# Reordering the low-rank adds of a gated-attention and channel-mixer kernel, and storing its last outputs singly

## The chip, the cores and the metric

The kernel runs on one core of a Trainium2 chip. A profile is one execution with every instruction's start and duration. PE is the matrix engine, DVE the vector engine, ACT the scalar engine, POOL and SP are engines that here mostly issue transfers. A label such as L545 is a line of the kernel's source.

## The reference, cut to what matters

For each of 8 batches of 3136 rows, with D = 256, a rank of 32 and 1024 hidden channels:

```python
scores = (1.0 / S) * z @ z.T
x = u * (np.maximum(scores, 0) ** 2 @ v)          # gated attention
h = (x.T @ U @ V).T                               # low-rank mix over rows
y = x + h
out = y + np.maximum(y @ w_ch1, 0) @ w_ch2        # channel mixer
```

## The kernel before: the parts concerned

A batch is done in 25 turns i of 128 rows (one of 64), two turns to an output pair. While batch b is in attention, the low-rank adds and the channel mixer of batch b - 1 are woven in. PSUM is the memory that the matmuls write and that DVE and ACT read here; a bank is one tile of 128 x 512 float32 in it. Four PSUM banks form two sets of two: an output pair accumulates in one set, and the low-rank product and the down matmuls use the other, until the next pair opens on it. Here are the low-rank add of one chunk (up to four tiles of rows), and the score, whose activation and square are queued by ACT and DVE when the matmuls are queued:

```python
def low_rank(b, c, ps=None, turned=True):
    ps = spare() if ps is None else ps            # the set that no pair accumulates in
    # ... two to four matmuls into ps[0], ps[1]                    (L531, PE)
    for h in range(2):                            # one add per bank
        # ...
        nc.vector.tensor_tensor(out=q, in0=split(ps[h][:, ...]), in1=q, op=ALU.add)   # L545, DVE
    if turned:
        turn_x(b, c)                              # DMA transpose, for the up matmuls

def score(b, parts):
    # ... two matmuls into one of two double banks                 (L298, PE)
    for dst, src in todo:
        nc.scalar.activation(out=dst, in_=src, func=AF.Relu, scale=sc)          # L311, ACT
    for dst, _ in todo:
        nc.vector.tensor_tensor(out=dst, in0=dst, in1=dst, op=ALU.mult)         # L313, DVE
```

The weaving of a turn, where `main` holds the 25 steps of one output tile (two matmuls each) and `fill` the scores that are due; `_spread` deals the fill out evenly between the steps:

```python
ahead = dict(zip((2, 3, 6, 7, 10, 11, 14), range(NC)))   # turn -> chunk
# ...
main = attend_steps(b, o)
if b and i in ahead:
    main.insert(17 if (i + (i > FIRST)) % 2 == 0 else 10, lambda c=ahead[i]: low_rank(b - 1, c))
_spread(main, fill)
```

Turn 7 has three scores; the second falls due after step index 12. The last batch has no following batch to hide in, so its ups, downs and low-rank adds stand at the end:

```python
rank(b, other[0], 0, NT - 3)
run(late[: NH // 2])                  # relus of the first chunk, alternating between bank sets
rank(b, other[0], NT - 3)
run(late[NH // 2 : NH // 2 + 1])
mix(b, 0)
run(late[NH // 2 + 1 :])
low_rank(b, 1, other)
for c in range(NC + 1):
    up, down = last[c]
    if c + 2 < NC:
        up.insert(3 if c == 0 else 1, lambda c=c: low_rank(b, c + 2, other))
    if c == 0:
        up.insert(1, lambda: low_rank(b, 0, None, False))
    run(_merge(up, down))
```

## Time and profile before

| | before |
|---|---|
| median time, first three runs | 1004.49 us (1002.80 to 1008.39) |
| median of all six runs of the first comparison | 1003.74 us |
| span of the profiled run, granted clock | 1003.0 us, 1.000 |
| PE idle in it | 18.8 us |
| shortest interval between two batches | 121.21 us |
| first last-batch rank matmul (L462) to start of the last relu | 50.80 us |
| start of the last relu to the end of the span | 6.57 us |

The last three rows are from the trace's instruction records, and they serve as rulers. The interval is that between the first L479 matmuls (the rank projection, once a batch) of neighbouring batches; the shortest of the six is free of stray waits.

### The profile page before, as it was taken

How to read it: one execution, taken by the hardware profiler on the slowest of the kernel's cores; microseconds unless marked ns; L12 is line 12 of the kernel's file. 1: busy time of each engine (PE TensorE's matmuls, PEld its weight loads, DVE VectorE, ACT ScalarE, POOL GpSimd, SP SyncE). 2: the span in 40 equal slices, each digit the busy share in tenths (PEclk: the TensorE clock that was granted, in tenths of full speed). 3: DMA queues.
4: the chain of work that ended last, by engine and by line, in shares of the span. 5: the costliest groups of instructions: out<-in, count | busy, mean ns of one | idle time of the engine just before them, and what ended most of it. 6: DMA issues, size and time to landing. Idle time of an engine off the chain costs nothing.

```text
span 1003.0 us, 31017 instructions
## 1 busy us (share of the span) xinstructions
PE 984.2 (98%) x13688; PEld 776.2 (77%) x13688; DVE 550.6 (55%) x1002; ACT 612.3 (61%) x835; POOL 171.8 (17%) x317
## 2 busy tenths in 40 slices
PE   7899999999999999999999999999999999999998
PEld 5678777787778877788787887778878788777855
DVE  6868754457544665456644566445663457542342
ACT  7877764667645776466755667466664667633154
POOL 5111112111121211221112211112111120011000
PEclk9999999999999999999999999999999999999999
DMA  9999989999798999999999997989989998678442
GB/s 177 186 196 206 175 153 186 169 198 173 149 205 165 170 160 181 178 179 168 156 185 174 188 162 149 192 177 179 170 156 181 181 183 152 127 152 166 99 98 97
DMA packets 414646, 167.94 MB, mean 167 GB/s; under 512 B 389472, under 2 KB 399136, under 8 KB 414512
## 3 DMA queue, kind: packets, MB, share of 16 engines
q1 hardware_dynamic: 385280, 99.68, 62.9%
q0 software_dynamic: 29232, 66.28, 28.5%
q8 instruction: 107, 1.75, 0.7%
q14 instruction: 27, 0.22, 0.1%
HBM read 61.88 MB, written 25.69 MB: 87 GB/s over the span
## 4 chain that ended last, share of the span: by engine, by line
PE 90%; DVE 4%; ACT 3%; DMA 2%; issue 0%; POOL 0%; DVEq 0%; ACTq 0%; POOLq 0%
PE ps L371 46%; PE ps L608 17%; PE ps L563 17%; PE ps L298 6%; ACT A L311 3%; DVE A L313 1%; PE ps L405 1%; DMA strip<-A 1%; DVE x_bf L545 1%; PE ps L531 1%; DMA z_c<-in_z_dram 1%; PE ps L479 1%; DMA zT<-z_bf 1%; DVE both L386 1%; DVE x_bf L395 0%
## 5 line engine op out<-in xcount | busy, mean ns | idle before, releaser
L311 ACT ACTIVATE A<-ps 128x832 bf16<-128x832 f32 (+9 forms) x477 | 359.1, 768 | 156.1 <-PE ps L298 149.6
L371 PE MATMUL ps<-v,A 64*128 64x256 bf16 x4988 | 341.8, 270 | 2.4 <-DVE A L313 1.1
L313 DVE TENSOR_TENSOR A<-A 128x832 bf16<-128x832 bf16 (+9 forms) x477 | 244.6, 527 | 131.2 <-ACT A L311 128.0
L371 PE MATMUL ps<-v,strip 64*128 64x256 bf16 x4420 | 307.4, 269 | 3.6 <-DMA strip<-A 2.7
L371 PEld LDWEIGHTS <-A 64*128 64x128 bf16 x4988 | 246.8, 94 | 45.8 <-issue 11.2
L581 ACT ACTIVATE relu_bf<-ps 128x1024 bf16<-128x1024 f32 (+2 forms) x206 | 186.0, 911 | 140.8 <-PE ps L563 138.7
L371 PEld LDWEIGHTS <-strip 64*128 64x128 bf16 x4420 | 222.8, 94 | 37.4 <-DMA strip<-A 4.6
L619 DVE TENSOR_TENSOR o_sb<-ps,x_bf 128x512 f32<-128x512 f32 (+1 forms) x104 | 69.7, 670 | 246.2 <-PE ps L608 223.8
L608 PE MATMUL ps<-w_bf,relu_bf 128*128 128x256 bf16 (+1 forms) x1600 | 201.5, 273 | 0.2 <-ACT relu_bf L579 0.2
L563 PE MATMUL ps<-ut,w_bf 128*128 128x512 bf16 (+2 forms) x896 | 198.3, 353 | 1.1 <-DVE x_bf L545 1.0
L608 PEld LDWEIGHTS <-relu_bf 128*128 128x128 bf16 (+1 forms) x1600 | 152.3, 98 | 46.6 <-issue 4.6
L563 PEld LDWEIGHTS <-w_bf 128*128 128x128 bf16 x896 | 85.0, 98 | 63.4 <-issue 7.7
L355 POOL DMA_DIRECT2D u_sb<-in_u_dram x96 | 53.7, 559 | 456.1 <-DVE x_bf L395 440.8
L298 PE MATMUL ps<-zT 64*128 64x416 bf16 (+8 forms) x812 | 131.7, 312 | 0.0
L385 ACT COPY both<-ps 128x512 f32<-128x512 f32 (+1 forms) x104 | 58.9, 566 | 73.8 <-PE ps L371 66.4
L632 POOL DMA_DIRECT2D out_dram<-o_sb x84 | 46.0, 548 | 278.2 <-DVE o_sb L619 274.9
L386 DVE TENSOR_TENSOR both<-ps,both 128x512 f32<-128x512 f32 (+1 forms) x104 | 69.4, 667 | 27.5 <-ACT both L385 26.7
L395 DVE TENSOR_TENSOR x_bf<-both,u_sb 128x512 bf16<-128x512 f32 (+1 forms) x104 | 69.8, 672 | 3.6
L545 DVE TENSOR_TENSOR x_bf<-ps,x_bf 128x512 bf16<-128x512 f32 (+1 forms) x112 | 65.4, 626 | 8.1 <-PE ps L531 8.0
L298 PEld LDWEIGHTS <-zT 64*128 64x128 bf16 x812 | 43.2, 94 | 3.9
L244 POOL DMA_DIRECT2D v<-in_v_dram x61 | 34.1, 561 | 1.2 <-DMA w_bf<-in_moe_w_ch_dram 1.1
L298 PE MATMUL ps<-relu_bf 64*128 64x416 bf16 (+9 forms) x121 | 22.2, 332 | 4.1 <-ACT A L311 3.3
(54 smaller groups left out, 207.9 us busy)
## 6 DMA issues: line engine op xcount, KB each, us to landing
u_sb<-in_u_dram POOLq DMA_DIRECT2D x96, 256.0 KB, 4.1
out_dram<-o_sb POOLq DMA_DIRECT2D x84, 256.0 KB, 3.2
v<-in_v_dram POOLq DMA_DIRECT2D x57, 192.0 KB, 5.1
strip<-A SPq DMA_TRANSPOSE x196, 5.6
out_dram<-o_sb SPq DMA_DIRECT2D x12, 256.0 KB, 2.0
z_c<-in_z_dram POOLq DMA_DIRECT2D x7, 384.0 KB, 5.7
u_sb<-in_u_dram POOLq DMA_DIRECT2D x16, 64.0 KB, 2.9
ut<-x_bf SPq DMA_TRANSPOSE x56, 3.6
```

The costliest lines, as they stand in the source:

```text
L298: mm(out=ps[:, k, :n], lhsT=zT[halves[k], j, :], rhs=zT_flat[halves[k], c : c + n], start=True, stop=True,)
L311: nc.scalar.activation(out=dst, in_=src, func=AF.Relu, scale=sc)
L313: nc.vector.tensor_tensor(out=dst, in0=dst, in1=dst, op=ALU.mult)
L371: mm(out=acc[t0][h][:, (o - t0) * D : (o - t0 + 1) * D], lhsT=w[halves[h]], rhs=v_both[b % 2][halves[h], j, :], start=start, stop=stop, **kw,)
L385: nc.scalar.copy(out=both[:, :w], in_=banks[1][:, :w])
L386: nc.vector.tensor_tensor(out=both[:, :w], in0=banks[0][:, :w], in1=both[:, :w], op=ALU.add)
L395: nc.vector.tensor_tensor(out=x_at(b, t0, n), in0=split(both[:, :w]), in1=u_sb[:, :n, :].rearrange("p t (a c) -> p t a c", c=P), op=ALU.mult,)
L545: nc.vector.tensor_tensor(out=q, in0=split(ps[h][:, : len(ks) * D]), in1=q, op=ALU.add)
L563: mm(out=ps[i][:, :w] if apart else ps[:, i, :w], lhsT=w1_bf[:, db, (hp + i) * P : (hp + i + 1) * P], rhs=uT[c][:, db, len(chunks[c]) * P ...
L581: nc.scalar.activation(out=relus[c][:, hp : hp + 2, :w], in_=ps[:, :, :w], func=AF.Relu)
L608: mm(out=ps[r, k * D : (k + 1) * D], lhsT=relus[c][:, ht, q : q + (TAIL if two else P)], rhs=w2_bf[:, ht, :], start=(ht < 1 + two), stop=( ...
L619: nc.vector.tensor_tensor(out=o_sb[:p, :nk, :].rearrange("p t (a c) -> p t a c", c=P), in0=split(ps[:p, : nk * D]), in1=x_at(b, t, nk)[:p] ...
```

## The change

Its intent: in the last batch, spread the low-rank adds so that they use one bank set (`other`) and stay out of the way of the first chunk's relus; let the last two output tiles leave one by one; and put the add of turn 7 later, away from the wait in front of it. The diff, cut to its core:

```diff
+        apart = b == B - 1 and c == NC - 1          # in down_steps
...
-            if k == len(pair) - 1:
-                t, nk = pair[0], len(pair)
-                o_sb = out_pool.tile([P, 2, D], FP32, name="o_sb")
+            if apart or k == len(pair) - 1:
+                k0 = k if apart else 0
+                t, nk = pair[k0], k + 1 - k0
+                if k0 == 0:
+                    hold[1] = out_pool.tile([P, 2, D], FP32, name="o_sb")
+                o_sb = hold[1][:, k0 : k + 1, :]
...
-                    in0=split(ps[:p, : nk * D]),
+                    in0=split(ps[:p, k0 * D : (k + 1) * D]),
...
-                main.insert(17 if (i + (i > FIRST)) % 2 == 0 else 10, lambda c=ahead[i]: low_rank(b - 1, c))
+                at = 17 if (i + (i > FIRST)) % 2 == 0 else 13 if i == 7 else 10
+                main.insert(at, lambda c=ahead[i]: low_rank(b - 1, c))
...
+    ups = NH // 2
     rank(b, other[0], 0, NT - 3)
-    run(late[: NH // 2])
+    run(late[: ups // 2])
     rank(b, other[0], NT - 3)
-    run(late[NH // 2 : NH // 2 + 1])
+    run(late[ups // 2 : ups])
     mix(b, 0)
-    run(late[NH // 2 + 1 :])
     low_rank(b, 1, other)
+    run(late[ups:])
     for c in range(NC + 1):
         up, down = last[c]
-        ...                                         # the inserts shown above
+        steps = _merge(up, down)
+        adds = {0: ((2, 2),), 1: ((0, 1), (3, 5))}.get(c, ((c + 2, 2),) if c + 2 < NC else ())
+        for n, at in reversed(adds):
+            steps.insert(at, lambda n=n: low_rank(b, n, other, n > 0))
+        run(steps)
```

More of the change, by code (lines that the diff above doesn't have):

```diff
@@ L614, in step @@
                 )
-            if k == len(pair) - 1:
-                t, nk = pair[0], len(pair)
-                o_sb = out_pool.tile([P, 2, D], FP32, name="o_sb")
+            if apart or k == len(pair) - 1:
[4 more added lines that the diff above has]
+                o_sb = hold[1][:, k0 : k + 1, :]
                 p = P if t < NF else TAIL
                 nc.vector.tensor_tensor(
-                    out=o_sb[:p, :nk, :].rearrange("p t (a c) -> p t a c", c=P),
-                    in0=split(ps[:p, : nk * D]),
+                    out=o_sb[:p].rearrange("p t (a c) -> p t a c", c=P),
+                    in0=split(ps[:p, k0 * D : (k + 1) * D]),
                     in1=x_at(b, t, nk)[:p],
@@ L631, in step @@
                 if t < NF:
-                    store(out=rows(out[b])[:, t : t + nk, :], in_=o_sb[:, :nk, :])
+                    store(out=rows(out[b])[:, t : t + nk, :], in_=o_sb)
                 else:
@@ L896 @@
     other = sets[opened[0] % 2]
+    ups = NH // 2
     rank(b, other[0], 0, NT - 3)
-    run(late[: NH // 2])
+    run(late[: ups // 2])
     rank(b, other[0], NT - 3)
-    run(late[NH // 2 : NH // 2 + 1])
+    run(late[ups // 2 : ups])
     mix(b, 0)
-    run(late[NH // 2 + 1 :])
     low_rank(b, 1, other)
+    run(late[ups:])
     for c in range(NC + 1):
         up, down = last[c]
-        if c + 2 < NC:
-            up.insert(3 if c == 0 else 1, lambda c=c: low_rank(b, c + 2, other))
-        if c == 0:
-            up.insert(1, lambda: low_rank(b, 0, None, False))
-        run(_merge(up, down))
+        steps = _merge(up, down)
[3 more added lines that the diff above has]
+        run(steps)
 _INS = ['u', 'v', 'z', 'moe_U', 'moe_V', 'moe_w_ch1', 'moe_w_ch2']
```

## The prediction

> **What bounds the kernel now.** I read the page's busy times and chain first.
>
> ```profile
> PE 984.2 (98%) x13688; PEld 776.2 (77%) x13688; DVE 550.6 (55%) x1002; ACT 612.3 (61%) x835; POOL 171.8 (17%) x317
> ...
> PE 90%; DVE 4%; ACT 3%; DMA 2%; issue 0%; POOL 0%; DVEq 0%; ACTq 0%; POOLq 0%
> ```
>
> The matrix engine (PE) is busy for 984.2 of 1003.0 us, and 90% of the chain is its matmuls. The change removes no matmul, so at most the 18.8 us of PE idleness (1.9%) is to be had. Hence I look only for moments where PE waits. The list of waits names one that repeats once in each of seven batches:
>
> ```profile
> PE ps L531 <- DVE x_bf L545: 1.1, 7, 0.2
> ```
>
> The timeline around the first of them (microseconds from the start, then duration):
>
> ```profile
> 138.39 1.28 DVE L545 TENSOR_TENSOR x_bf<-ps,x_bf 128x512 bf16<-128x512 f32 x2
> ...
> 139.30 0.27 PE L531 MATMUL ps<-t_sb,V_bf 64*128 64x256 bf16 x1
> ...
> 139.72 0.28 PE L531 MATMUL ps<-t_sb,V_bf 64*128 64x256 bf16 x2 [0.16 <-DVE x_bf L545]
> ...
> 140.05 0.33 PE L298 MATMUL ps<-zT 64*128 64x352 bf16 x2
> ...
> 140.19 1.02 DVE L545 TENSOR_TENSOR x_bf<-ps,x_bf 128x512 bf16<-128x512 f32 x2
> ...
> 140.42 0.76 ACT L311 ACTIVATE A<-ps 128x704 bf16<-128x704 f32 x1 [0.71 <-PE ps L298]
> ...
> 141.21 0.96 DVE L313 TENSOR_TENSOR A<-A 128x704 bf16<-128x704 bf16 x2
> ...
> 141.56 0.72 PE L371 MATMUL ps<-v,A 64*128 64x256 bf16 x10
> ```
>
> L531 is the low-rank product of chunk 3 of the previous batch, at turn i = 7. It writes the pair of PSUM banks that the accumulation is not using. Its second matmul waits until the vector engine (DVE) has read the previous low-rank result out of its bank (L545, ends 139.67). Three such matmuls take about 0.22 us elsewhere; here 0.54 us pass (139.30 to 139.84), so 0.32 us are lost. Note the last line: at 141.56 the next output pair (i = 8) opens **the same two banks**. Its matmuls also wait for L545, which ended at 141.21: a margin of 0.35 us.
>
> The last batch is the other place. From the chain of waits, in order of time:
>
> ```profile
> 949.02 0.39 ACT relu_bf L579
> ...
> 952.00 0.68 DVE o_sb L619
> 952.68 0.91 DVE x_bf L545 x2
> 953.59 0.20 issue
> 953.79 0.69 DVE x_bf L545
> 954.49 0.04 issue
> 954.53 0.59 PE ps L563 x2
> ...
> 998.96 0.69 DVE o_sb L619
> ```
>
> Between 947 and 955 us the chain leaves PE for relus and adds. The largest hole is before 954.53: chunk 0's second relu pair (L563) needs the banks into which low_rank(0) has just been put, and DVE reaches its two adds after three others. From 958 us on PE is packed. At the end one 0.69 us add is followed by the last store.
>
> **What the Trainium skill says.** "PSUM — Partial Sum Buffer", section "Engine vs sequencer instructions": VectorE queues are strict FIFO, and matmuls start and complete in program order. The trace agrees: at 139.72 the third L531 matmul, whose bank was free, waited behind the second. "VectorE: DVE Perf Modes", section "The TRN2 errata": a fixed cost per instruction, and (N+151)/0.96 ns for an fp32 tensor_tensor. The trace has 0.69 us for 512 columns and 0.42 us for the 64x256 output add, which is what that gives; half an add is not half the time. "DMA: Bandwidth & Descriptors", section "Latency and other measured facts": about 2 us of fixed cost per DMA. The 256 KB stores land 2.0 us after issue, and the DMA view of the last 7 us shows the engines moving data for about 0.8 us of that, so size matters less than the fixed part. "Perfetto Trace Analysis", section "Identifying the Most-Contended Engine", says that matmul busy time is a poor measure of headroom; I use it only to locate gaps, and issue starts for sizes.
>
> **The change part by part.** I read the order of instructions per engine in both built programs.
>
> *Part 1, spread low-rank adds (last batch).* The same matmuls and adds stand in another order. Walk, with durations of the trace (four 512-column matmuls 0.86 us, eight L608 0.87, a low-rank group with its changes of shape 0.42). The last ranks move between the two halves of chunk 0's first relus, so the t1 copy comes earlier and the 0.27 us wait at 949.19 to 949.46 shrinks; the mix issues at 949.2 instead of 950.4. low_rank(1) follows it; then sixteen down matmuls run from 949.85 (relu ends about 949.80) to 951.6, and chunk 0's up starts there instead of 952.14. Its second pair finds bank 0 free and bank 1 free once the output add ends (about 952.7), before PE comes at 952.9. So the hole before 954.53 goes. Chunk 1's up starts at about 955.45 instead of 957.71, but with one low-rank group (0.42) still to do, and the third one later as before. The start of chunk 2 comes to 963.2 against 965.13: **1.9 us saved**. A 0.14 us wait at 973.8 also goes, since d3 now stands before the next chunk's up. Sum -2.0 us.
>
> *Part 2, last outputs singly.* The last add takes 0.42 instead of 0.69 us (-0.27); the last store is 128 KB instead of 256 KB (half of about 0.7 us of moving, so -0.3). One more add and store lie beside the last eight matmuls (0.87 us). Sum about -0.55 us.
>
> *Part 3, the add at i = 7 moved from step 10 to 13.* The order shows what the diff does not: the score A 128x704 (L298, L311, L313), which stood after the low-rank matmuls, now stands just before them **on DVE too**. Gain: the matmuls come 0.47 us later (139.77), after 139.67, so 0.32 us is saved. Cost: without that wait L298 issues at 139.62 (three pairs of 0.107 after 139.30). The activation ran 0.38 us behind its matmul and takes 0.76: 140.00 to 140.76. The square starts 0.03 later, 140.79, and the next DVE instruction starts 0.44 behind such a square (139.75 to 140.19): L545 runs from 141.23 to 141.92 and, 0.60 after its start, from 141.83 to 142.25. Before, it ended at 141.21. PE would open pair i = 8 at 141.57 - 0.32 = 141.25, its two first matmuls together; now the second bank is free at about 142.30. So a new wait of about 1.05 us replaces the old 0.32: **+0.72 us a batch**. Nothing near it in a steady batch absorbs this: the waits of PE in 480 to 602 us are this one and 3.5 us of changes of shape. Seven batches: +5.0 us.
>
> Total: -2.0 - 0.55 + 5.0 = +2.4 us.
>
> **Rivals.** (a) *Part 3 pays.* If PE kept working at the opening of i = 8, the seven waits would go: -2.2 us, and in all 999.7 us. For it: whoever moved the add meant to clear this wait, and step 12, just ahead of the score, would have done so. Against: DVE is in order, both banks are awaited, and the margin of 0.35 us is smaller than the 1.04 us by which L545 ends later. (b) *The transpose takes the place of the removed wait.* Chunk 1's transposed input is issued at the end of its adds and took 3.1 us to land. I get adds done at 952.06 and landing at 955.2, with PE there at 955.45: 0.25 us of margin. A landing of 4.7 us, which also occurs in this stretch, would cost 1.4 us: then 1008. (c) *The tail is hidden anyway*: the last store's fixed cost does not shrink, and part 2 gives only 0.27: 1007.2.
>
> **Range and chances.** 1004.5 + 2.4 = 1006.9. The three runs of before spread from 1002.8 to 1008.4, and (a) pulls down, so I take 1006.5, with 1002.0 to 1009.5. A change over 2% needs 20 us; PE's whole idle time is 18.8, and the costs are of a few us: 0.98 for within 2%.
>
> **What would show it.** Step 3: in the waits, PE L531 <- L545 gone (7 times), and PE L371 <- DVE x_bf L545 new, 7 times, total some 7 us by issue starts. Part 1: chunk 2's up in the last batch 1.9 us earlier relative to the end of the attention, no PE hole of 1 us after 953. Part 2: last DVE add 0.42 us. I am wrong if L371 shows no wait at i = 8, in which case the time falls below 1001, or if a wait for the transpose opens near 955.

## More of the kernel before

The metric is device time in microseconds (us), taken as the median of several runs.

In the changed kernel the output add and the down matmuls have moved by a few lines: L608 became L610, L619 became L624, L632 became L637.

The down step of a pair of output tiles accumulates both tiles in the two halves of one bank; after the second, one add (L619) reads both and one store leaves.

The end of the kernel before, from its timeline (start, duration, engine, line, and in brackets the idle time before and what ended it):

```profile
996.13 2.78 PE L608 MATMUL ps<-w_bf,relu_bf 128*128 128x256 bf16 x24
996.40 0.60 ACT L581 ACTIVATE relu_bf<-ps 128x512 bf16<-128x512 f32 x1 [0.71 <-PE ps L563]
...
998.96 0.69 DVE L619 TENSOR_TENSOR o_sb<-ps,x_bf 128x512 f32<-128x512 f32 x1 [1.05 <-PE ps L608]
```

The last 24 down matmuls run as one block, then one add of 512 columns; the store and its completion take the time to 1003.0.

## The result, and the profile after

The changed kernel takes 1007.41 us in the median (1005.87 to 1008.55, six runs) against 1003.74 us: the same within 2%, and slightly slower. The ratio is 1.003, with a 95% interval of 1.0009 to 1.005. A ratio is the mean time of one kernel's fast runs over that of the other's in the same rounds, so it isn't quite the ratio of the medians. The profiled run spans 1005.6 us at a clock of 0.998.

The waits of PE in the changed kernel, with total, times and longest. The line of L531 that the prediction shows is gone; these two are new:

```profile
PE ps L371 <- DVE x_bf L545: 3.8, 7, 0.5
...
PE ps L610 <- DVE o_sb L624: 0.5, 1, 0.5
```

Here is the same stretch of turn 7 as in the prediction, in the changed kernel:

```profile
138.22 1.28 DVE L545 TENSOR_TENSOR x_bf<-ps,x_bf 128x512 bf16<-128x512 f32 x2
...
139.45 0.31 PE L298 MATMUL ps<-zT 64*128 64x352 bf16 x2
...
139.60 0.38 PE L531 MATMUL ps<-t_sb,V_bf 64*128 64x256 bf16 x3
...
139.81 0.76 ACT L311 ACTIVATE A<-ps 128x704 bf16<-128x704 f32 x1 [0.27 <-PE ps L298]
...
140.60 0.53 DVE L313 TENSOR_TENSOR A<-A 128x704 bf16<-128x704 bf16 x1 [0.50 <-ACT A L311]
...
141.04 1.01 DVE L545 TENSOR_TENSOR x_bf<-ps,x_bf 128x512 bf16<-128x512 f32 x2
...
141.78 1.03 PE L371 MATMUL ps<-v,A 64*128 64x256 bf16 x10 [0.54 <-DVE x_bf L545]
```

Read it from the top. The three low-rank matmuls now run without a break (0.38 us in one row). But the score L298 stands ahead of them, so DVE, which works in order, waits 0.50 us for the score's activation, squares it, and only then comes to the two adds. These end at 142.06. The opening of the next pair wants their banks: PE started its last matmul before that at 140.97 and the next two at 141.78 and 142.11, where such starts otherwise follow by 0.107 and 0.02 us. That makes (0.81 - 0.11) + (0.33 - 0.02) = 1.01 us lost. The bracket shows only 0.54 because the idle time is counted from a modelled end of the matmul before; **for a stalled matmul, read the distance between starts**. The pattern is the same in all seven batches.

The end of the changed kernel:

```profile
998.74 1.91 PE L610 MATMUL ps<-w_bf,relu_bf 128*128 128x256 bf16 x16
999.00 0.60 ACT L581 ACTIVATE relu_bf<-ps 128x512 bf16<-128x512 f32 x1 [0.71 <-PE ps L563]
...
1000.69 0.42 DVE L624 TENSOR_TENSOR o_sb<-ps,x_bf 128x256 f32<-128x256 f32 x1 [0.18 <-PE ps L610]
1001.16 1.03 PE L610 MATMUL ps<-w_bf,relu_bf 128*128 128x256 bf16 x8 [0.51 <-DVE o_sb L624]
1002.24 0.42 DVE L624 TENSOR_TENSOR o_sb<-ps,x_bf 128x256 f32<-128x256 f32 x1 [1.13 <-PE ps L610]
```

The block of 24 is broken: the last eight matmuls wait for the first tile's add, which reads the other half of the bank that they write.

### The profile page after: what moved, and what is told of

The parts are those of the page before. It is cut to its first block, busy times and chain, and to the rows that moved or that the text cites. A ratio compares the mean times of both kernels' runs of the same rounds, so it can differ in the third digit from the quotient of the medians.

```text
span 1005.6 us, 30980 instructions
## 1 busy us (share of the span) xinstructions
PE 984.7 (98%) x13648; PEld 776.2 (77%) x13688; DVE 550.6 (55%) x1003; ACT 612.2 (61%) x835; POOL 171.7 (17%) x317
## 4 chain that ended last, share of the span: by engine, by line
PE 91%; DMA 3%; ACT 3%; DVE 2%; issue 0%; POOL 0%; DVEq 0%; ACTq 0%; POOLq 0%
PE ps L371 48%; PE ps L610 17%; PE ps L563 17%; PE ps L298 6%; ACT A L311 2%; PE ps L405 1%; DMA strip<-A 1%; PE ps L531 1%; DMA zT<-z_bf 1%; DVE x_bf L545 1%; DMA z_c<-in_z_dram 1%; DVE A L313 1%; PE ps L479 1%; PE ps L462 0%; DVE o_sb L624 0%
## 5 line engine op out<-in xcount | busy, mean ns | idle before, releaser
L624 DVE TENSOR_TENSOR o_sb<-ps,x_bf 128x512 f32<-128x512 f32 (+2 forms) x105 | 69.8, 665 | 243.5 <-PE ps L610 228.3
L563 PE MATMUL ps<-ut,w_bf 128*128 128x512 bf16 (+2 forms) x856 | 196.3, 352 | 2.1
L298 PE MATMUL ps<-zT 64*128 64x416 bf16 (+8 forms) x812 | 133.6, 312 | 0.0
L563 PEld LDWEIGHTS <-w_bf 128*128 128x128 bf16 x896 | 85.0, 98 | 61.9 <-issue 6.7
L298 PEld LDWEIGHTS <-zT 64*128 64x128 bf16 x812 | 45.0, 94 | 4.2
L298 PE MATMUL ps<-relu_bf 64*128 64x416 bf16 (+9 forms) x121 | 21.9, 335 | 4.1 <-ACT A L311 3.3
```

What stands on the lines that cost most here:

```text
L298: mm(out=ps[:, k, :n], lhsT=zT[halves[k], j, :], rhs=zT_flat[halves[k], c : c + n], start=True, stop=True,)
L563: mm(out=ps[i][:, :w] if apart else ps[:, i, :w], lhsT=w1_bf[:, db, (hp + i) * P : (hp + i + 1) * P], rhs=uT[c][:, db, len(chunks[c]) * P ...
L624: nc.vector.tensor_tensor(out=o_sb[:p].rearrange("p t (a c) -> p t a c", c=P), in0=split(ps[:p, k0 * D : (k + 1) * D]), in1=x_at(b, t, nk) ...
```

## The experiments

My theory is three separate effects: +0.69 us in each of seven batches, about -2 us from the spread adds, and nothing from the single outputs. The table has all runs, with the rulers of their traces (us).

| kernel | median | before | ratio (95%) | batch | rank to last relu | last relu to end |
|---|---|---|---|---|---|---|
| before | 1003.74 | | | 121.21 | 50.80 | 6.57 |
| changed | 1007.41 | 1003.74 | 1.0030 (1.0009 to 1.0050) | 121.90 | 48.81 | 6.61 |
| e1_move_only | 1008.80 | 1005.04 | 1.0042 (1.0015 to 1.0069) | 121.90 | 50.79 | 6.57 |
| e2_no_move | 1003.04 | 1005.04 | 0.9977 (0.9951 to 1.0003) | 121.20 | 48.81 | 6.60 |
| e3_ahead_of_score | 999.69 | 1005.04 | 0.9943 (0.9922 to 0.9965) | 120.88 | 48.82 | 6.62 |
| e4_adds_first | 1000.63 | 1005.04 | 0.9960 (0.9932 to 0.9988) | 120.88 | 48.82 | 6.62 |
| e5_no_single | 1006.69 | 1006.84 | 0.9995 (0.9959 to 1.0031) | 121.89 | 48.81 | 6.57 |
| e6_two_banks | 1006.67 | 1006.84 | 1.0000 (0.9963 to 1.0037) | 121.90 | 48.82 | 6.01 |
| e7_both | 1000.28 | 1006.84 | 0.9930 (0.9896 to 0.9964) | 120.87 | 48.81 | 6.01 |
| e8_adds_late | 1010.31 | 1006.84 | 1.0030 (0.9997 to 1.0063) | 122.34 | 50.79 | 6.57 |
| r1_changed | 1006.15 | 1004.67 | 1.0013 (0.9988 to 1.0039) | 121.90 | 48.81 | 6.61 |
| r2_adds_late | 1011.61 | 1004.67 | 1.0067 (1.0042 to 1.0093) | 122.34 | 50.79 | 6.58 |
| r3_both | 998.71 | 1004.67 | 0.9937 (0.9910 to 0.9964) | 120.87 | 48.81 | 6.00 |

### e1: the move of the turn-7 add alone

```diff
 # the kernel before
-                main.insert(17 if (i + (i > FIRST)) % 2 == 0 else 10, lambda c=ahead[i]: low_rank(b - 1, c))
+                at = 17 if (i + (i > FIRST)) % 2 == 0 else 13 if i == 7 else 10
+                main.insert(at, lambda c=ahead[i]: low_rank(b - 1, c))
```

> Kernel before with part 3 alone (the add at turn 7 moved from step 10 to 13, ahead on nothing, behind the score on the vector engine). Theory (the score's square delays the two adds, and the next pair's opening waits for them): about 1.0 us of new wait and 0.32 us removed in each of seven batches, so +4.8 us against the kernel before; the profile shows PE L371 waiting for the adds L545 seven times. Rival A (the move pays, the loss of the changed kernel is in the last batch): -2.2 us. Rival B (what differs is the granted clock, 0.998 against 1.000, not the order): about 0.

(The words "ahead on nothing" in it are a slip.) Slower: 1.0042. The batch takes 121.90 us, as in the changed kernel, and the two rulers of the last batch are those of the kernel before. So the loss is all in this one line. The granted clock isn't the cause: r1 has batches of 121.90 at a clock of 1.000, where the kernel before has 121.21.

### e2: all but the move

```diff
 # the changed kernel
-                at = 17 if (i + (i > FIRST)) % 2 == 0 else 13 if i == 7 else 10
+                at = 17 if (i + (i > FIRST)) % 2 == 0 else 10
```

> Changed kernel with part 3 undone (the add at turn 7 back at step 10). Theory: parts 1 and 2 are left, -1.9 us from the spread adds and about 0 from the single outputs (their gain of 0.27 to 0.5 us is eaten by a wait of the last eight matmuls for the first half's add): -2.0 us against the kernel before. Rival A: parts 1 and 2 lose, +2 us or more.

Its median is 2.0 us below that of the kernel before; the interval just includes 1. The trace is sharper: batch as before, 1.99 us less between rank and last relu, nothing at the end.

### e3: the add later, but ahead of the score

```diff
 # the changed kernel; the add is done inside step 12, so the score after that step comes behind it
-                at = 17 if (i + (i > FIRST)) % 2 == 0 else 13 if i == 7 else 10
-                main.insert(at, lambda c=ahead[i]: low_rank(b - 1, c))
+                at = 17 if (i + (i > FIRST)) % 2 == 0 else 10
+                if i == 7:
+                    step12 = main[12]
+                    main[12] = lambda c=ahead[i]: (step12(), low_rank(b - 1, c))
+                else:
+                    main.insert(at, lambda c=ahead[i]: low_rank(b - 1, c))
```

> Changed kernel, with the low-rank add of turn 7 after step 12 but ahead of the score instead of behind it: its matmuls come 0.32 us later than in the kernel before. Theory: PE finds both banks free (they are free at 139.73 in the time of the kernel before, the second matmul comes at 139.63, so at most 0.1 us of wait), the adds end when they ended before, and no wait appears at the opening of the next pair: 0.3 us saved in seven batches, -2.2 us, with parts 1 and 2 -4.2 us against the kernel before. Rival C (any later place of the add uses up the margin of 0.35 us at the opening): some 0.3 us a batch lost again, so no gain over undoing the move, -2 us or worse.

The fastest of its call, 0.9943. The batch takes 120.88 us, 0.33 less than before, which is the old wait of 0.32. Neither the old nor the new wait is in its list. Turn 7 in its timeline:

```profile
138.89 0.39 PE L531 MATMUL ps<-t_sb,V_bf 64*128 64x256 bf16 x3
...
139.45 1.02 DVE L545 TENSOR_TENSOR x_bf<-ps,x_bf 128x512 bf16<-128x512 f32 x2
...
140.38 0.72 DVE L313 TENSOR_TENSOR A<-A 128x704 bf16<-128x704 bf16 x2
...
140.52 0.71 PE L371 MATMUL ps<-v,A 64*128 64x256 bf16 x10
```

So the intent of the move was right, and one place earlier it would have worked: what decides is whether the add or the score's square comes first.

### e4: PE's order of the changed kernel, the adds ahead of the square on DVE

```diff
 # the changed kernel: the second score of turn 7 hands back its square, and the add queues it
...                                                 # cut: how it is handed back
+                def add(c=ahead[i]):
+                    low_rank(b - 1, c)
+                    if holding:
+                        for squares in holding.pop():
+                            squares()
-                main.insert(at, lambda c=ahead[i]: low_rank(b - 1, c))
+                main.insert(at, add)
...
```

> Changed kernel with the very same order of matmuls on PE, but on the vector engine the two adds of turn 7 stand ahead of the score's square. Theory: the wait at the opening vanishes, though PE's order is unchanged: -1.0 us in seven batches against the changed kernel, so about -4 us against the kernel before. Rival C (the later place on PE makes the wait): the wait stays, about +3 us against the kernel before.

The built program has the same matmuls in the same order as the changed kernel (all 13688 weight loads, one for each matmul, come in the same order in both traces). Its timeline at turn 7 (lines 7 further down here: L538 is the low-rank matmul, L552 its add, L315 the square, L378 the attention matmul):

```profile
140.21 0.38 PE L538 MATMUL ps<-t_sb,V_bf 64*128 64x256 bf16 x3
...
140.63 1.02 DVE L552 TENSOR_TENSOR x_bf<-ps,x_bf 128x512 bf16<-128x512 f32 x2
...
141.57 0.72 DVE L315 TENSOR_TENSOR A<-A 128x704 bf16<-128x704 bf16 x2
141.69 0.72 PE L378 MATMUL ps<-v,A 64*128 64x256 bf16 x10
```

The adds come first, the opening at 141.69 has no bracket, and the batch takes 120.88 us, 1.02 less than in the changed kernel. So the later place on PE doesn't make the wait; the place in DVE's queue does.

### e8: PE's order of the kernel before, the adds behind the square on DVE

```diff
 # the kernel before: low_rank can hand back its two adds and the transpose
...                                                 # cut: the handing back, into held
+                if i == 7:
+                    score1 = fill[1]
+                    fill[1] = lambda: (score1(), held[0]())
```

> Kernel before with PE's order unchanged (add at step 10), but on the vector engine the two adds of turn 7 stand behind the score's square. Theory (the place on the vector engine makes the wait at the opening): the old wait of 0.32 us stays and about 1.1 us of new wait comes at the opening of the next pair in each of seven batches: +8 us against the kernel before, worse than the change itself. Rival C (the later matmuls on PE make the wait): about 0.

Here the matmuls stay where they were (again all weight loads come in one order) and only DVE's order is turned round:

```profile
139.45 0.29 PE L531 MATMUL ps<-t_sb,V_bf 64*128 64x256 bf16 x2 [0.15 <-DVE x_bf L547]
...
140.94 0.53 DVE L313 TENSOR_TENSOR A<-A 128x704 bf16<-128x704 bf16 x1 [0.93 <-ACT A L311]
...
141.38 1.02 DVE L547 TENSOR_TENSOR x_bf<-ps,x_bf 128x512 bf16<-128x512 f32 x2
...
142.12 1.03 PE L371 MATMUL ps<-v,A 64*128 64x256 bf16 x10 [0.65 <-DVE x_bf L547]
```

The old wait is there and the new one too, and the batch takes 122.34 us, 1.13 more than before. That should give 7 x 1.13 = 7.9 us. The ratio said only 1.003, because the kernel before ran from 1002.56 to 1012.59 us. So I ran this kernel again, with the changed one beside it (r2 and r1, below).

### e5 and e6: the single outputs

```diff
 # e5, from the changed kernel
-        apart = b == B - 1 and c == NC - 1
+        apart = False
 # e6, from the changed kernel: the second tile goes to the other bank of the set
-            if k == 0:
-                hold[0] = spare()[1 - n]
+            if k == 0 or apart:
+                hold[0] = spare()[1 - n - k]
```

> Changed kernel with part 2 undone (the last pair of outputs leaves together again). Theory (part 2 is worth nothing, because the last eight matmuls wait about 0.5 us for the first half's add, which reads the bank they write): from the start of the last relu to the end of the span 6.6 us, as in the kernel before and in the changed one; time within noise of the changed kernel, +3 us against the kernel before. As predicted on record (part 2 saves 0.55 us): 0.5 us longer after the last relu than the changed kernel.

> Changed kernel with the second of the two single outputs computed in the other PSUM bank of the pair. Theory (the shared bank makes the wait): the wait of PE L610 for the first half's add is gone, and from the start of the last relu to the end of the span 6.1 us instead of 6.6. Rival D (the store's fixed cost or the add itself sets the end): 6.6 us still. The whole time moves by 0.5 us only, inside the noise: +2.5 us against the kernel before.

In whole times the two are level (1006.69 and 1006.67 us); half a microsecond is inside the scatter. The last stretch tells: 6.57 us without single outputs, 6.61 with them, 6.01 with two banks. All traces agree: 6.57 or 6.58 in the other four without, 6.60 to 6.62 in the other four with them in one bank, 6.00 and 6.01 in the other two with two banks. The end of e6:

```profile
998.48 2.85 PE L610 MATMUL ps<-w_bf,relu_bf 128*128 128x256 bf16 x24
998.74 0.60 ACT L581 ACTIVATE relu_bf<-ps 128x512 bf16<-128x512 f32 x1 [0.71 <-PE ps L563]
...
1000.43 0.42 DVE L624 TENSOR_TENSOR o_sb<-ps,x_bf 128x256 f32<-128x256 f32 x1 [0.18 <-PE ps L610]
1001.38 0.42 DVE L624 TENSOR_TENSOR o_sb<-ps,x_bf 128x256 f32<-128x256 f32 x1 [0.52 <-PE ps L610]
```

The 24 matmuls are one block again. Storing singly is worth 0.6 us when the two tiles lie in different banks, and nothing when they share one. A bank is also one tile of the program here, so the runs don't tell whether the program's semaphores guard it as a bank or as a tile.

### e7: the add ahead of the score and the two banks together

The edits of e3 and e6 in the changed kernel.

> The spread low-rank adds, the add of turn 7 ahead of the score, and two banks for the last two outputs. Theory: the sum, about -5.7 us (measured without the two banks) and -0.5 us: -6 us against the kernel before, the fastest of all. Rival: the gains overlap, and it is no faster than without the two banks.

0.993, faster than the kernel before, with both rulers as in e3 and e6. Against e3 the gain of the two banks (0.6 us) is visible in the trace alone.

### r1, r2, r3: three kernels side by side on one chip

The changed kernel, e8 and e7 again, without an edit.

> The changed kernel again, on one chip with the next two, because the kernel before ran from 1002.6 to 1012.6 us in the last call. Theory, summed from the traces: seven times 0.69 us of longer batch, 1.99 us less in the last batch, 0 at the end: +2.8 us against the kernel before.

> The kernel before with the two adds of turn 7 behind the score's square, again. Theory: each batch is 1.13 us longer in its trace, so +7.9 us, clearly above the changed kernel. The last call's ratio (1.003) would be a matter of its slow runs of the kernel before; if it is +3 us again, the batch period of one profile is no measure of the whole time.

> Spread adds, the add of turn 7 ahead of the score, two banks for the last two outputs, again. Theory: seven times 0.33, 1.99 and 0.6 us less: -4.9 us against the kernel before and -7.7 us against the changed kernel of this call.

Among each other the three stand as the traces say: e8 is 5.5 us above the changed kernel (expected 7.9 - 2.8 = 5.1), and e7 7.4 us below it (expected 7.7). Against the kernel before each ratio lies lower than summed (1.0067 and 1.0013 in place of some 1.008 and 1.003), in part because the kernel before had long runs: plain means without its runs of 1012.21 and 1014.37 us give 1.0075 and 1.0021. So e8 is clearly slower (though within 2%), and the doubt is gone.

What those long runs are is not settled. Those of the kernel before from 1012 to 1014 us show a granted clock of 0.995 to 0.997, but two of its runs at 1005.0 and 1006.8 us show 0.996 as well. In the profile of the kernel before DVE waits for an earlier store to free an output buffer, five times and up to 4.8 us, and PE waits behind one of them; e7's second profile has six such waits and two batches that are 2.0 and 2.8 us longer. A third output buffer would test this, but the kernel doesn't build with one (its buffers no longer find room), so it was not run.

## Why the prediction was right

The time, 1007.41 us, is inside the range of 1002.0 to 1009.5 and 0.9 us from the number given; the sign of the change was right as well. That the miss is so small is partly luck: the base, 1004.5, was 0.8 us above the later median of the kernel before, and the change from it, put at +2.0 after leaning towards (a), was measured at +3.7 between the medians. By its steps:

- **Part 3, the add at turn 7: right.** It said 0.32 us saved and 1.05 us of new wait in each of seven batches. Measured: 1.01 us of new wait, and a batch 0.69 us longer (+0.72 was said). Counted from the start of the adds of the low-rank group before it, which stand first in both stretches, the two adds ended 1.02 us later than before (142.06 - 138.22 = 3.84 against 141.21 - 138.39 = 2.82). e4 and e8 show the mechanism by itself.
- **Part 1, the spread adds: right.** It said -2.0 us; rank to last relu went from 50.80 to 48.81, -1.99. The hole before the second relu pair is gone: in the chain of the changed kernel the ups of the first chunk follow each other.

```profile
956.62 1.46 PE ps L563 x6
958.07 0.33 PE ps L531 x4
958.40 2.70 PE ps L563 x12
961.10 0.32 PE ps L531 x4
```

- **Part 2, the single outputs: wrong.** It said -0.55 us; the last stretch went from 6.57 to 6.61. The step that failed is "One more add and store lie beside the last eight matmuls": they don't, because both tiles share a bank and PE waits 0.51 us for the add. The terms themselves were near: the add took 0.42 us, as said, and the halved store landed in 1.8 instead of 2.0 us (-0.2, where -0.3 had been counted). With two banks (e6) the last stretch is 0.56 us shorter than in the kernel before, which is the size predicted. The Trainium skill would have told: "PSUM — Partial Sum Buffer", section "PSUM bank collisions raise a hardware error", has as its rule to guard PSUM with semaphores by bank and quadrant (by bank in the simple version), not by address; the 0.51 us wait of matmuls that write other columns than the add reads agrees. In the trace the first of the eight matmuls carries this wait on DVE's semaphore, so it stood in the built program and could have been read there.
- **Rivals.** (a), that the move pays, fell with e1. It is true of the place ahead of the score, as that rival itself noted: e3. (b), the transpose: it was issued at 956.67 and landed 3.1 us later, at 959.74, and chunk 1's up came at 960.07 (the ninth of the twelve L563 from 958.33), so nothing waited. The margin was 0.33 us, where 0.25 had been estimated. (c) gave the nearest size for part 2, but for another reason: the store's time did shrink, and the wait ate the gain.

The sum, 7 x 0.69 - 1.99 = +2.8 us with the last stretch left at zero, stands against +3.7 in the medians, +3.0 by the ratio and +2.6 between the two profiled spans; the rest is within the scatter of the runs.

## What to carry to other kernels

Before moving work to dodge a wait, look at what it comes to stand behind on the *other* engines: a bank is free only when the engine that reads it has worked through all that was queued ahead, and here one square, whose input wasn't ready, cost three times what the move saved. Find the next user of the same buffer and its margin (0.35 us here) and compare it with the delay. To let a part of a result leave early, give it its own PSUM bank; in this kernel its reader otherwise stopped the writer of the rest for 0.51 us.

## What the Trainium skill lacked or had wrong

- "PSUM — Partial Sum Buffer", section "Engine vs sequencer instructions", states that the queues are strict FIFO, but no page draws the consequence for freeing a bank: turning round the square and the two adds on DVE alone, with PE's order untouched, changed the batch by 1.02 us (e4) and 1.13 us (e8).
- "TensorE: Matmul & The Clock Gate", section "Back-to-back issue gap", gives about 131 ns a matmul for streams of weight load and matmul with N = 512, and about 216 ns for the isolated case. In this kernel every matmul has its own weight load, and twelve of 512 columns took 2.70 us of the chain, 225 ns each; the starts within such a group are 0.216 us apart. The isolated figure fits and the sustained one doesn't.
- "Perfetto Trace Analysis", section "Optimization Strategy", tells to find the gaps between slices on the engine in question. The page itself calls PE's end times estimated, but doesn't say that gaps suffer from it. In these profiles they undercount: the gap read 0.54 us where the distance between starts shows 1.01 us lost, over two matmuls.
